# Two pairs' last score chunks on four 64x64 tiles, and the seventh group's q squared before its k

## The chip, the cores and the metric

One core of one Trainium2 chip. The metric is device microseconds of one execution of the whole kernel; times are medians over several executions, with the lowest and highest behind them. The profile shows one of these executions from inside; its span is 1.8 us shorter than that execution's time. TensorE's granted clock is reported for each execution: 1.00 is full speed, and one stretch of about 3.4 us at half speed lowers the mean of a 587 us span by about 0.003. A "hole" is a stretch in which TensorE starts nothing; the profile's own count of it (idle time, in square brackets) is 0.1 to 0.2 us shorter than the distance from start to start less the usual distance, and the text says which one it means where that matters.

## The reference

Cosine attention of 8 batches x 12 heads x 448 positions x 64, then a low-rank token mixer with a channel mixer of two matmuls.

```python
q_n = q / (norm(q) + 1e-6);  k_n = k / (norm(k) + 1e-6)
attn = softmax(q_n @ k_n.T / tau)
x = heads_side_by_side(attn @ v)              # 8 x 448 x 768
u = x + ((x.T @ U) @ V).T                     # U 448x32, V 32x448
return u + relu(u @ w_ch1) @ w_ch2            # 768 -> 3072 -> 768
```

## The kernel before

Heads go through in 48 pairs, 0 to 47, two heads of 64 side by side in 128 partitions. Pairs 0 to 5 are the first batch. q, k and v are loaded in groups of one or two pairs; the seventh group holds pairs 10 and 11, the eighth pairs 12 and 13, the ninth 14 and 15, the tenth 16 and 17. A group is squared on GpSimd, reduced and inverted on VectorE, and scaled to bf16; from pair 12 on the scaled q and k are transposed by DMA instead of by TensorE. After the start nearly all loads, stores and transposes go out from one queue, SyncE's; the mixer's weights (w1 and w2, of `w_ch1` and `w_ch2`) are issued by GpSimd. The code is shortened: arguments shown as `...` and the calls that only keep count of time (`est`) are left out.

```python
def step_T(b, p):
    if not by_dma(b * NP + p):                # by_dma: pair >= 12
        pe_T(b, p); evict_T(b, p); return
    gi, j = group_of[(b, p)]
    nc.sync.dma_start_transpose(out=new_qkT(b, p)..., in_=norm[gi][0][:, j, ...]...)

def pe_S(b, p, c):                            # scores, chunk c of the keys
    sc = psum.tile([128, 2, 512], FP, name="sc", tag="ps_sc", bufs=2)
    if c == 3:                                # last: 64 keys of each head, one wide matmul
        nc.tensor.matmul(out=sc[:, 0, 0:S], lhsT=t[:, 1, 384:512], rhs=t[:, 0, 0:S], ...)
        return
    for h in range(2):                        # two row tiles side by side
        r = slice(64 * h, 64 * h + 64)
        nc.tensor.matmul(out=sc[:, h, 0:S], lhsT=t[r, 1, c * 128:(c + 1) * 128], rhs=t[r, 0, 0:S], ...)
# (cut)
for gi in range(5, len(groups)):
    # at: the places (pair, step) of square q, square k, cast v, reduce q, reduce k, root
    # when: of the inversion and the four scalings
    elif m == NP + 4:                         # the seventh group
        at = [(NP + 2, 0), (NP + 2, 0), (NP + 2, 6), (NP + 2, 3), (NP + 2, 4), (NP + 2, 5)]
        when = [(NP + 2, 6), (NP + 2, 6), (NP + 3, 0), (NP + 3, 2)]
    # (cut)
    put(*at[1], lambda g=g: g.square(1))      # k
    put(*at[0], lambda g=g: g.square(0))      # q; same place: stays behind k
    # (cut)
    put(m - 6, 4, lambda gi=gi: load(gi, "q", nc.sync))
    put(m - 5, 5, lambda gi=gi: load(gi, "k", nc.sync))
    put(m - 4, 3, lambda gi=gi: load(gi, "v", nc.sync))
    if by_dma(m):
        put(m - 1, -1 if m > 2 * NP else 2, lambda m=m: T(m))
        put(m - 1, 0 if m > 2 * NP else 4, lambda m=m: T(m + 1))
```

## Time and profile before

| | before |
|---|---|
| time, median of 3 (range) | 590.51 us (589.85 to 591.66) |
| span of the profiled execution | 587.6 us |
| TensorE busy | 574.8 us, 98% |
| longest hole of TensorE | 2.65 us from start to start (2.49 idle), at 69.2 to 71.9 us, then 3.4 us at half clock |
| wide last-chunk matmuls | 48, each 0.19 us from start to start |

TensorE is the bound, so time is read as a sequence of TensorE starts: work removed shortens it, and so does a hole removed, as long as nothing further on stops TensorE at a fixed moment.

### The profile page before, as it was taken

What the parts mean: (1) busy time and instruction counts of PE and PEld (TensorE: products, weight loads), DVE (VectorE), ACT (ScalarE), POOL (GpSimd) and SP (SyncE); (2) the same over time, 40 slices, a digit from 0 to 9 for tenths busy, and PEclk for the clock granted to TensorE, in tenths of its full rate; (3) what the DMA queues carried; (4) which work ended last, traced back from release to release, by engine and by line L of the source; (5) the groups of instructions that cost most, each with busy time, mean ns of one, the idle gap of its engine ahead of it and who ended that gap; (6) DMA issues with size and microseconds to landing.
All of it is one profiled execution on the core that took longest, in us unless ns stands there. A gap on an engine that the chain in (4) does not pass through costs nothing.

```text
span 587.6 us, 11561 instructions
## 1 busy us (share of the span) xinstructions
PE 574.8 (98%) x4729; PEld 328.9 (56%) x4729; DVE 254.3 (43%) x500; ACT 263.6 (45%) x452; POOL 187.8 (32%) x160
## 2 busy tenths in 40 slices
PE   7999899999999999999999999999999999999997
PEld 6665456655555555554555555655555545555564
DVE  7875644534444437425344255633355242220011
ACT  5966455356324555346433465345442465214300
POOL 9674456504135045224053153252251410000000
PEclk9999999999999999999999999999999999999999
DMA  6999999456275464574565763773545631222022
GB/s 165 204 227 233 240 236 227 119 117 135 73 162 139 107 145 113 132 162 108 94 151 121 157 132 86 147 162 85 135 108 133 131 65 26 56 61 46 7 48 55
DMA packets 138581, 74.20 MB, mean 126 GB/s; under 512 B 85568, under 2 KB 138352, under 8 KB 138528
## 3 DMA queue, kind: packets, MB, share of 16 engines
q1 hardware_dynamic: 128256, 62.77, 47.3%
q0 software_dynamic: 9728, 10.18, 10.2%
q8 instruction: 37, 0.61, 0.4%
q10 hardware_dynamic: 544, 0.51, 0.3%
q14 instruction: 16, 0.13, 0.1%
HBM read 52.19 MB, written 11.01 MB: 108 GB/s over the span
## 4 chain that ended last, share of the span: by engine, by line
PE 89%; DMA 6%; DVE 1%; SPq 1%; ACT 1%; issue 0%; DVEq 0%; ACTq 0%; POOLq 0%
PE mp L512 38%; PE mp L485 34%; PE sc L318 5%; PE av L356 3%; DMA qst<-in_q_dram 3%; PE up L356 2%; DMA kst<-in_k_dram 2%; PE sc L312 1%; DMA vst<-in_v_dram 1%; PE av L349 1%; PE up L349 1%; PE up L442 1%; PE av L455 1%; PE tp L288 1%; ACT E L329 0%
## 5 line engine op out<-in xcount | busy, mean ns | idle before, releaser
L512 PE MATMUL mp<-w_sb,relu 128*128 128x384 bf16 x1344 | 236.1, 326 | 0.0
L512 PEld LDWEIGHTS <-relu 128*128 128x128 bf16 x1344 | 125.4, 98 | 91.3 <-issue 14.3
L485 PEld LDWEIGHTS <-w_sb 128*128 128x128 bf16 x1152 | 107.6, 98 | 101.5 <-issue 10.5
L329 ACT ACTIVATE E<-sc 128x896 bf16<-128x896 f32 x144 | 124.6, 916 | 65.4 <-PE sc L318 64.8
L489 ACT ACTIVATE relu<-mp 128x448 bf16<-128x448 f32 x167 | 90.9, 544 | 136.6 <-PE mp L485 136.6
L259 POOL TENSOR_TENSOR qk<-kst,inv 128x512 bf16<-128x512 f32 x41 | 49.6, 1226 | 259.5 <-DVE inv L253 259.5
L485 PE MATMUL mp<-uE,w_sb 128*128 128x448 bf16 x576 | 119.8, 354 | 0.0
L485 PE MATMUL mp<-uO,w_sb 128*128 128x448 bf16 x576 | 115.6, 353 | 0.0
L530 DVE TENSOR_TENSOR o_sb<-mp,ut 128x384 f32<-128x384 f32 x50 | 27.8, 556 | 122.6 <-PE mp L512 122.6
L239 DVE TENSOR_REDUCE ss<-sq 128x16 f32<-128x1024 f32 (+1 forms) x50 | 56.8, 1165 | 3.5 <-POOL sq L234 2.8
L367 DVE RECIPROCAL rd<-av 128x4 f32<-128x4 f32 x54 | 9.7, 181 | 90.9 <-PE av L356 90.9
L234 POOL TENSOR_TENSOR sq<-kst 128x1024 f32<-128x1024 f32 (+1 forms) x23 | 43.9, 1912 | 13.3 <-DMA kst<-in_k_dram 6.8
L259 DVE TENSOR_TENSOR qk<-qst,inv 128x512 bf16<-128x512 f32 x42 | 45.7, 1094 | 0.5
L356 PEld LDWEIGHTS <-E 128*128 128x128 bf16 x1152 | 45.0, 97 | 0.0
L234 POOL TENSOR_TENSOR sq<-qst 128x1024 f32<-128x1024 f32 x21 | 42.8, 2040 | 5.0 <-DMA qst<-in_q_dram 5.0
L318 PE MATMUL sc<-qkT 64*128 64x448 bf16 x288 | 41.7, 358 | 1.2 <-ACT E L326 0.6
L326 ACT ACTIVATE E<-sc 128x448 bf16<-128x448 f32 x48 | 26.0, 541 | 28.7 <-PE sc L312 28.7
L267 POOL CAST v<-vst 128x1024 bf16<-128x1024 f32 (+1 forms) x25 | 28.5, 1142 | 13.1 <-DMA vst<-in_v_dram 7.6
L491 DVE TENSOR_SCALAR relu<-mp 128x448 bf16<-128x448 f32 x25 | 15.6, 623 | 33.8 <-PE mp L485 33.5
L356 PE MATMUL av<-v,E 128*128 128x65 bf16 x648 | 29.1, 193 | 0.0
L349 PEld LDWEIGHTS <-E 128*128 128x128 bf16 x192 | 17.9, 98 | 15.3 <-DVE uO L460 0.8
L367 DVE RECIPROCAL rd<-up 128x4 f32<-128x4 f32 x36 | 6.5, 182 | 44.9 <-PE up L356 44.9
(93 smaller groups left out, 328.3 us busy)
## 6 DMA issues: line engine op xcount, KB each, us to landing
out_dram<-o_sb SPq DMA_DIRECT2D x109, 96.0 KB, 2.2
w_sb<-in_moe_w_ch_dram POOLq DMA_DIRECT2D x8, 1152.0 KB, 26.2
qst<-in_q_dram SPq DMA_DIRECT2D x23, 256.0 KB, 4.0
vst<-in_v_dram SPq DMA_DIRECT2D x46, 128.0 KB, 2.7
kst<-in_k_dram SPq DMA_DIRECT2D x44, 128.0 KB, 2.7
qst<-in_q_dram SPq DMA_DIRECT2D x23, 192.0 KB, 4.0
vst<-in_v_dram SPq DMA_DIRECT2D x46, 96.0 KB, 2.6
kst<-in_k_dram SPq DMA_DIRECT2D x44, 96.0 KB, 2.7
```

Of the source, the lines that this page charges most:

```text
L234: nc.gpsimd.tensor_mul(sq[:, 0:self.nh * 4, :], self.flat(t), self.flat(t))
L239: nc.vector.reduce_sum(self.ss[:, j, 0:self.nh * 4], self.sq[j][:, 0:self.nh * 4, :], axis=AX.X)
L259: eng.tensor_mul(qks[self.gi % 2][:, j, i, :, :, :], t[:, 2 * j:2 * j + 2, :, :].rearrange("p h c d -> p c h d"), iv.unsqueeze(3).to_broad ...
L267: nc.gpsimd.tensor_copy(out=self.flat(v65[self.s])[:, :, 0:D], in_=self.flat(vst[self.s]))
L318: nc.tensor.matmul(out=sc[:, h, 0:S], lhsT=t[r, 1, c * 128:(c + 1) * 128], rhs=t[r, 0, 0:S], start=True, stop=True)
L329: nc.scalar.activation(out=e[:, 2 * c:2 * c + 2, 0:S], in_=sc[:, :, 0:S], func=AF.Exp)
L349: nc.tensor.matmul(out=av[:, i, :, :], lhsT=e[:, 6, ic * 128:(ic + 1) * 128], rhs=vv[:, 2 * j:2 * j + 2, 3, :], start=(i == 0), stop=False ...
L356: nc.tensor.matmul(out=av[:, i, h, :], lhsT=e[:, 2 * c + h, ic * 128:(ic + 1) * 128], rhs=vv[:, 2 * j + h, c, :], start=False, stop=(i == ...
L485: nc.tensor.matmul(out=mp, lhsT=w1_sb[:, cc, f * 128:(f + 1) * 128], rhs=u[:, cc, 0:S], start=(cc == 0), stop=(cc == CC - 1))
L489: nc.scalar.activation(out=relu[:, f, o:o + S], in_=mp, func=AF.Relu)
L512: nc.tensor.matmul(out=mp, lhsT=relu[:, f, r0:r0 + 128], rhs=w2_sb[:, f, half * HC:(half + 1) * HC], start=(f == 0), stop=(b > 0 and f == ...
L530: nc.vector.tensor_add(o.rearrange("p (k d) -> p k d", d=128), mp.rearrange("p (k d) -> p k d", d=128), ut_of[(b, half)][:, :, c, :])
```

## The change

Three things. From pair 14 on, the last score chunks of two pairs are computed together by four 64x64 matmuls on the four quarters of the array, in two banks (separate pieces) of PSUM, the memory that TensorE writes to, instead of one wide matmul for each pair. So that each head's last keys lie on the right partitions, k and v of the middle two heads of a group are loaded mirrored. And the seventh group's q is squared first, its k second.

```diff
+    def step_S3(b, p):
+        for i, (nm, tag) in enumerate((("av", "ps_av"), ("up", "ps_x"))):
+            t = qkT[(b, p + i)]
+            bank = psum.tile([128, 512], FP, name=nm, tag=tag, bufs=1)
+            sc_of[(b, p + i, 3)] = bank.unsqueeze(1)
+            for h in range(2):
+                r, o = slice(64 * h, 64 * h + 64), 64 * (h ^ i)
+                nc.tensor.matmul(out=bank[o:o + 64, 0:S], lhsT=t[r, 1, 384 + o:448 + o],
+                                 rhs=t[r, 0, 0:S], start=True, stop=True)
+        # (cut)
+        for i in range(2):
+            exp_S(b, p + i, 3)
# (cut: order of an even pair's steps)
             order = [
+                (2, now and (lambda: (step_S3(*pairs[n]), Sc(n, 0, 1)))),
                 (2, lambda: V(n - 1, 0)),
-                (2, now and (lambda: Sc(n, 0, 1))),
                 (2, lambda: (V(n - 1, 1), X2(n - 1))),
-                (2, now and (lambda: Sc(n, 3))),
# (cut: the seventh group)
-            at = [(NP + 2, 0), (NP + 2, 0), (NP + 2, 6), (NP + 2, 3), (NP + 2, 4), (NP + 2, 5)]
-            when = [(NP + 2, 6), (NP + 2, 6), (NP + 3, 0), (NP + 3, 2)]
+            at = [(NP + 2, 0), (NP + 2, 1), (NP + 2, 6), (NP + 2, 3), (NP + 2, 5), (NP + 2, 6)]
+            when = [(NP + 3, 0), (NP + 3, 0), (NP + 3, 1), (NP + 3, 3)]
# (cut: a buffer E3 for the exponentials of the last chunks, with its own fills of ones on
#  GpSimd; mirrored loads; V_raw under another tag; two reciprocal buffers instead of four)
```

More of the change, by code (lines that the diff above doesn't have):

```diff
@@ L98 @@
         for lst in (kst, vst):
-            nc.vector.memset(lst[i][64:128, 0:NG:2, 3, :], 0.0)
-            nc.vector.memset(lst[i][0:64, 1:NG:2, 3, :], 0.0)
+            nc.vector.memset(lst[i][64:128, 0:NG:3, 3, :], 0.0)
+            nc.vector.memset(lst[i][0:64, 1:3, 3, :], 0.0)
     ident = const.tile([128, 128], BF, name="ident")
@@ L104, with last_of @@
         nc.gpsimd.memset(t[:, :, :, D:D + 1], 1.0)
-        nc.gpsimd.memset(t[64:128, 0:NG:2, 3, D:D + 1], 0.0)
-        nc.gpsimd.memset(t[0:64, 1:NG:2, 3, D:D + 1], 0.0)
-    E = []
+        nc.gpsimd.memset(t[64:128, 0:NG:3, 3, D:D + 1], 0.0)
+        nc.gpsimd.memset(t[0:64, 1:3, 3, D:D + 1], 0.0)
+    E, E3 = [], []
     for i in range(2):
-        t = const.tile([128, 7, 512], BF, name=f"E{i}")
+        t = const.tile([128, 6, 512], BF, name=f"E{i}")
         nc.gpsimd.memset(t[:, :, S:512], 1.0)
         E.append(t)
+        t = const.tile([128, 2, 512], BF, name=f"E3{i}")
+        nc.gpsimd.memset(t[:, :, S:512], 1.0)
+        E3.append(t)
+    def last_of(b, p):
+        n = b * NP + p
+        return E3[n // 2 % 2][:, n % 2, :]
     U_raw = const.tile([128, 4, R], FP, name="U_raw")
     U_sb = const.tile([128, 4, 128], BF, name="U_sb")
-    V_raw = work.tile([128, S], FP, name="V_raw", tag="XT", bufs=2)
+    V_raw = work.tile([128, S], FP, name="V_raw", tag="ut", bufs=2)
     A_sb = [const.tile([128, 128], BF, name=f"A_sb{i}") for i in range(2)]
@@ L200, in load @@
         x, t = (k, kst[s]) if what == "k" else (v, vst[s])
-        ev, od = slice(h0, h0 + nh, 2), slice(h0 + 1, h0 + nh, 2)
-        engs[0].dma_start(out=dst(t, L, slice(0, nh, 2), 4), in_=src(x, ev, 0, 256, 4))
-        engs[1].dma_start(out=dst(t, U2, slice(0, nh, 2), 3), in_=src(x, ev, 256, 448, 3))
-        engs[2].dma_start(out=dst(t, L, slice(1, nh, 2), 3), in_=src(x, od, 0, 192, 3))
-        engs[3].dma_start(out=dst(t, U2, slice(1, nh, 2), 4), in_=src(x, od, 192, 448, 4))
+        m = min(3, nh)
+        ou, mi = slice(h0, h0 + nh, 3), slice(h0 + 1, h0 + m)
+        engs[0].dma_start(out=dst(t, L, slice(0, nh, 3), 4), in_=src(x, ou, 0, 256, 4))
+        engs[1].dma_start(out=dst(t, U2, slice(0, nh, 3), 3), in_=src(x, ou, 256, 448, 3))
+        engs[2].dma_start(out=dst(t, L, slice(1, m), 3), in_=src(x, mi, 0, 192, 3))
+        engs[3].dma_start(out=dst(t, U2, slice(1, m), 4), in_=src(x, mi, 192, 448, 4))
     norm = {}
@@ L320, in pe_S @@
         est.pe(0.25)
+    def step_S3(b, p):
[7 more added lines that the diff above has]
+                                 rhs=t[r, 0, 0:S], start=True, stop=True)
+        est.pe(0.19)
+        for i in range(2):
+            exp_S(b, p + i, 3)
     def exp_S(b, p, c):
@@ L325, in exp_S @@
         if c == 3:
-            nc.scalar.activation(out=e[:, 6, 0:S], in_=sc[:, 0, 0:S], func=AF.Exp)
+            nc.scalar.activation(out=last_of(b, p)[:, 0:S], in_=sc[:, 0, 0:S], func=AF.Exp)
             est.act(0.56)
@@ L348, in pe_V @@
             ic = 2 * half + i
-            nc.tensor.matmul(out=av[:, i, :, :], lhsT=e[:, 6, ic * 128:(ic + 1) * 128],
+            nc.tensor.matmul(out=av[:, i, :, :], lhsT=last_of(b, p)[:, ic * 128:(ic + 1) * 128],
                              rhs=vv[:, 2 * j:2 * j + 2, 3, :],
@@ L365, in divide_V @@
         av = av_of[(b, p, half)][:, 0:4 * (D + 1)].rearrange("p (i h d) -> p i h d", i=2, h=2)
-        rd = work.tile([128, 4, 1], FP, name="rd", tag="rd", bufs=4)
+        rd = work.tile([128, 4, 1], FP, name="rd", tag="rd", bufs=2)
         nc.vector.reciprocal(out=rd, in_=av.rearrange("p i h d -> p (i h) d")[:, :, D:D + 1])
@@ L793 @@
             order = [
+                (2, now and (lambda: (step_S3(*pairs[n]), Sc(n, 0, 1)))),
                 (2, lambda: V(n - 1, 0)),
-                (2, now and (lambda: Sc(n, 0, 1))),
                 (2, lambda: (V(n - 1, 1), X2(n - 1))),
-                (2, now and (lambda: Sc(n, 3))),
+                (2, None),
                 (3, lambda: (A2(n - 2), now and (Sc(n, 2), Sc(n + 1, 0)))),
@@ L816 @@
             (2, lambda: V(n - 1, 0)),
-            (2, lambda: Sc(n, 3)),
+            (2, None if n > FIRST2 + 1 else (lambda: Sc(n, 3))),
             (2, lambda: (V(n - 1, 1), X2(n - 1))),
```

## The prediction

> **What bounds the kernel now.** I read the first part of the page (busy shares), then the costliest groups, then the TensorE timeline of one late pair of heads, then the waits, then the stretches with their clock. The page's first part, and two of its groups:
>
> ```profile
> span 587.6 us, 11561 instructions
> PE 574.8 (98%) x4729; PEld 328.9 (56%) x4729; DVE 254.3 (43%) x500; ACT 263.6 (45%) x452; POOL 187.8 (32%) x160
> ...
> L318 PE MATMUL sc<-qkT 64*128 64x448 bf16 x288 | 41.7, 358 | 1.2 <-ACT E L326 0.6
> ...
> L312 PE MATMUL sc<-qkT 128*128 128x448 bf16 x48 | 16.9, 353 | 0.6 <-ACT E L329 0.6
> ```
>
> TensorE is busy 98% of the span, every other engine under half. So only two things can move the end: TensorE work taken out, and the 12.8 us (587.6 - 574.8) in which it waits. The mean of 353 ns for L312 is the latency of one matmul, not its price: matmuls are pipelined, so the price is the distance from one start to the next. The TensorE timeline of a late even pair shows it (start, length, count):
>
> ```profile
> 380.84 0.81 PE L512 MATMUL mp<-w_sb,relu 128*128 128x384 bf16 x4
> 381.49 0.35 PE L312 MATMUL sc<-qkT 128*128 128x448 bf16 x1
> 381.68 2.11 PE L512 MATMUL mp<-w_sb,relu 128*128 128x384 bf16 x12
> ...
> 386.49 0.55 PE L318 MATMUL sc<-qkT 64*128 64x448 bf16 x4
> 386.88 0.35 PE L455 MATMUL av<-V_sb,A_sb 64*128 64x448 bf16 x1
> 386.88 0.35 PE L455 MATMUL up<-V_sb,A_sb 64*128 64x448 bf16 x1
> 387.16 1.15 PE L512 MATMUL mp<-w_sb,relu 128*128 128x384 bf16 x6
> ```
>
> The wide last-chunk matmul takes 0.19 us (381.49 to 381.68). Two row-tiled ones at L455 start together and the next wide one follows after 0.28 us. Over all such places in the trace, medians of start to start: wide to wide 162 ns at 384 columns and 189 ns at 448; wide to a 64-row form 259 and 285 ns, so 96 ns more; 64-row to wide 282 ns, about 95 more than the 186 ns from one 64-row pair to the next (L318 to L455); from the 128x32 form (L442) to the 64-row form 152 ns, again 96 more than its 56. Every change of tile form costs 96 ns, staying in one costs nothing.
>
> The waits and the DVE, GpSimd and TensorE timelines around the one long hole give the second point:
>
> ```profile
> PE av L389 <- DVE X L368: 2.5, 1, 2.5
> ...
> 70.05 1.22 DVE L239 TENSOR_REDUCE ss<-sq 128x16 f32<-128x1024 f32 x1 [2.76 <-POOL sq L234]
> 71.19 0.17 DVE L367 RECIPROCAL rd<-av 128x4 f32<-128x4 f32 x1
> 71.39 0.42 DVE L368 TENSOR_TENSOR X<-av,rd 128x256 bf16<-128x256 f32 x1
> ...
> 66.28 1.89 POOL L234 TENSOR_TENSOR sq<-kst 128x1024 f32<-128x1024 f32 x1 [6.40 <-DVE rd L367]
> 68.13 1.88 POOL L234 TENSOR_TENSOR sq<-qst 128x1024 f32<-128x1024 f32 x1
> ...
> 68.08 1.30 PE L485 MATMUL mp<-uE,w_sb 128*128 128x448 bf16 x6
> 71.87 0.58 PE L389 MATMUL av<-X,U_sb 128*128 128x128 bf16 x4 [2.49 <-DVE X L368]
> ```
>
> ```profile
> 69.20:71.90 2.70, 0.21 (x2) 0.03 (x1) 1.81 (x4) 0.55 (x1) 1.85 (x2) 1.00 1.22 239
> 71.90:75.30 3.40, 3.40 (x17) 1.57 (x17) 1.58 (x3) 2.42 (x5) 0.99 (x1) 0.50 1.22 242
> ```
>
> Backward: the matmul at 71.87 waits for X, X stands in VectorE's queue behind the reduction of squared q, that waits for GpSimd's square of q, which comes second, after the square of k. The second fence (stretch, length, busy times, granted clock, DMA) shows what follows: the 2.7 us hole, then 3.4 us at clock 0.50. The "DVE rd" named before the square of k at 66.28 I do not believe: the transfers of k were issued at 51.3 to 55.5 and took 10.6 us or more to land, so the last lands at 66.1; the second q transfer, issued at 49.80, took 12.6 and was there at 62.4. The square waited for k while q lay ready. Excess of start to start over the normal distance, summed from 71.87 to 75.4: 2.65 us hole plus 1.4 us of half clock, 4.05 us. It is the eighth pair's stretch, and the squares are the seventh group's. Besides the start (first 41 us) there are no other holes over 0.6 us.
>
> **What the skill says.** "TensorEngine Tiling (Array Packing)", Key Properties: changing the tiling mode drains TensorE, changing the tile does not; the trace agrees, 96 ns against none. "TensorE: Matmul & The Clock Gate", Part 3 (The mechanism): tiles run concurrently, starts about 4 ns apart; here L318's two tiles start 4 ns apart (median). The same page, Part 1 (What's actually happening): after an idle window of about 3.4 us the clock halves; here 2.65 us of waiting were followed by 3.4 us at 0.50. "PSUM — Partial Sum Buffer", PSUM bank collisions: column tiles may write one bank at once, row tiles may not, measured there per bank and 32-partition quadrant. No run so far shows two row tiles in one bank on different partitions, which is what the change does.
>
> **The change part by part.**
> 1. Last chunks. Pairs 14 to 47, 34 of 48, lose their wide matmul: 34 x 189 ns = 6.43 us less. Instead 17 times four 64x64 matmuls for two pairs, each on its own tile. If they stream together as L318's pairs do, 186 ns + 3 x 4 = about 0.20 us: 17 x 0.20 = 3.4 us more. They stand directly before the first two chunks of scores (64x128), so the visit wide to 64-row to wide becomes wide to 64x64 to 64x128 to wide: one form change more, 17 x 96 ns = 1.6 us. Sum: -6.4 + 3.4 + 1.6 = -1.4 us. All of it is on TensorE, thus on the path.
> 2. The exponentials of these chunks stay 34 of 541 ns on ScalarE (45% busy), but two now come together ahead of two of 917 ns, about 3.0 us in a row. The first attention-times-values product now needs the bank that the first of them reads: it comes after about 0.5 us of scores and one mixer step of 1.0 to 1.1 us, 1.8 us after the new matmuls; the exponential is over at about 0.35 + 0.54 = 0.9 us, or 1.4 with a 0.54 us relu ahead. Nothing added.
> 3. The transposed q and k of the second pair are needed one pair earlier. The transposes are issued 5.7 us or more ahead of an even pair's start and take 3.1 to 5.5 us to land: just enough.
> 4. Mirrored middle heads: the same transfers with other head steps; nothing. V_raw in another buffer, two reciprocal buffers instead of four: nothing. The ones columns take four GpSimd fills instead of two: from fills of 448, 384 and 128 elements (468, 444, 205 ns) 0.36 us more at GpSimd's start, where it works without a gap until 14 us; I take 0.2 us for the span.
> 5. Seventh group, q first: q's square can run 62.4 to 64.3, before VectorE is at its reduction (free at 67.3). Reduction to 68.5, then the division, 0.6 us: X at 69.1, and TensorE comes to it at 69.2. The hole goes and with it the half clock: -4.05 us. k's square stays at about 66.2 to 68.1, its reduction is moved later by one place. What follows comes 4 us earlier into a time of loaded DMA (to about 97 us): w2's pieces landed 78.8, 88.7 and 95.2 us against first uses, shifted, of about 82, 98 and 100, enough; but pair 12's transpose was just in time before (issued 97.3, used at 101.3 with a small wait) and would now be issued near 93 among other transfers. I take +0.5 us.
>
> Sum: -1.4 + 0.2 - 4.05 + 0.5 = -4.75 us, from 590.5 to 585.8. So the larger part should come from the smallest edit, the order of two squares.
>
> **The rivals.**
> A. Tiles in one bank serialise. Then a visit is two passes of 0.19 us: 17 x 0.19 = 3.2 us more, the first part turns from -1.4 to +1.8, the time is 589. For it: the skill's sentence on row tiles and banks. Against it: the partitions differ, and each half of a bank gets one tile at a time. 10%.
> B. The step from 64x64 to 64x128 costs nothing, since the rows stay 64: another -1.6 us, 584.2. The trace shows only that 128x32 to 64x128 costs 96 ns, where both dimensions change. 20%.
> C. New waits: the values product waits for the exponential, or the mixer's banks for relus behind 3 us of exponentials. For it: two more buffers tied to ScalarE; against: the estimates in 2, and that VectorE can take relus. 0.2 us at 17 places would be 3.4 us, time 589. 10%.
> D. The hole stays, since the wait was for VectorE as the profile names it, or the transfers land later: 590. 10%.
>
> **Range and chances.** 2% is 11.8 us, more than twice what all parts give together, and no rival loses that much. Both gains full with B and no late transpose: 583.7; one of A, C or D: 588 to 590. Prediction 585.8, range 583.4 to 588.4. Faster by over 2%: 1%; within 2%: 98%; slower: 1%.
>
> **What would show it.** In the new trace: the four 64x64 starts within about 12 ns, the next 64x128 start some 290 ns after them (190 if B, near 480 if A); 14 L312-like matmuls left; TensorE busy less by some 3 us (1.4 from the tiles, 1.4 from the clock); no stretch at clock 0.50 near 72 us; the square of q starting near 62.4 and no wait of the X product over 0.3 us. I am wrong if the hole is still there, if it moves to pair 12's transpose or to 97 us with over 1 us, or if waits of TensorE for exponentials sum to over 1 us.

## The result, and the profile after

| | before | after |
|---|---|---|
| time beside each other, median of 4 (range) | 590.18 us (589.67 to 591.66) | 589.29 us (588.49 to 589.51) |
| span of the profiled execution | 587.6 | 586.7 |
| TensorE busy | 574.8 | 571.8 |

The ratio is 0.9978 (95%: 0.9957 to 0.9999). A ratio is the mean time of one kernel's fast runs over that of the other's in the same rounds, so not quite the ratio of the medians. The interval only just leaves out 1. The change gains 0.9 us where 4.75 were predicted, and 589.29 lies outside the range of 583.4 to 588.4.

The head of the page after. TensorE is busy 3.0 us less, and yet the span is only 0.9 us shorter, so it waits more than before (14.9 us instead of 12.8):

```profile
span 586.7 us, 11660 instructions
PE 571.8 (97%) x4763; PEld 327.2 (56%) x4763; DVE 259.4 (44%) x503; ACT 260.9 (44%) x449; POOL 187.7 (32%) x162
```

The tiles in the TensorE timeline after (start, length, engine, line, operation, count). The four 64x64 matmuls of L340 stream together, two banks 10 ns apart in these rounded starts, and the 64x128 scores of L328 follow 0.31 us later:

```profile
400.95 0.38 PE L340 MATMUL av<-qkT 64*64 64x448 bf16 x2
400.96 0.38 PE L340 MATMUL up<-qkT 64*64 64x448 bf16 x2
401.27 0.55 PE L328 MATMUL sc<-qkT 64*128 64x448 bf16 x4
```

The place of the old hole: the X product (L413) now starts at 71.64 directly behind the mixer step, without a wait. GpSimd squares q at 62.73, and k when it has landed, at 66.96. The stretch that held the hole (length, busy times of TensorE, weight loads, VectorE, ScalarE and GpSimd, granted clock, DMA share, GB/s) is full:

```profile
70.51 1.30 PE L509 MATMUL mp<-uE,w_sb 128*128 128x448 bf16 x6
71.64 0.39 PE L413 MATMUL av<-X,U_sb 128*128 128x128 bf16 x4
```

```profile
62.73 1.89 POOL L244 TENSOR_TENSOR sq<-qst 128x1024 f32<-128x1024 f32 x1 [3.00 <-DVE rd L391]
66.96 1.89 POOL L244 TENSOR_TENSOR sq<-kst 128x1024 f32<-128x1024 f32 x1 [2.34 <-DVE uO L443]
```

```profile
69.20:71.90 2.70, 2.70 (x31) 1.73 (x29) 2.67 (x5) 1.04 (x3) 1.04 (x1) 1.00 1.24 237
28.70:32.10 3.40, 3.40 (x32) 2.47 (x31) 1.41 (x4) 1.86 (x4) 1.95 (x2) 0.52 1.12 258
```

The second of these stretches shows that the half clock is not gone: it now lies at 28.7 to 32.1. It follows a hole at the start, where the first product of attention and values of pair 2 waits for the cast of v (TensorE, then GpSimd, before):

```profile
25.41 0.29 PE L349 MATMUL av<-v,E 128*128 128x130 bf16 x2
```

```profile
23.48 1.03 POOL L267 CAST v<-vst 128x1024 bf16<-128x1024 f32 x1 [3.17 <-DMA vst<-in_v_dram]
```

and after, where the same v landed at 26.0 instead of 23.3 us:

```profile
27.21 0.28 PE L373 MATMUL av<-v,E 128*128 128x130 bf16 x2 [1.65 <-POOL v L277]
```

```profile
26.13 1.03 POOL L277 CAST v<-vst 128x1024 bf16<-128x1024 f32 x1 [5.61 <-DMA vst<-in_v_dram]
```

And at pair 12. Before, its first scores (L318) follow the matmul ahead of them without a stop. The transposes that they need were issued at 97.33 (the queue of SyncE), and the view of their line gives the time from issue to landing:

```profile
100.95 0.35 PE L414 MATMUL up<-V_sb,A_sb 128*128 128x448 bf16 x1
101.28 0.55 PE L318 MATMUL sc<-qkT 64*128 64x448 bf16 x4
```

```profile
97.33 2.75 SPq L303 DMA_TRANSPOSE qkT<-qk  x2
```

```profile
DMA to landing us min/median/max: 3.3/3.6/3.9
```

After, TensorE is there at 99.5, 1.8 us earlier, and stands still until 101.61. The transposes were issued 1.8 us earlier too, at 95.53, behind loads of v and q, and took 2.1 us longer to land (the same three views):

```profile
99.15 0.35 PE L438 MATMUL up<-V_sb,A_sb 128*128 128x448 bf16 x1
101.61 0.55 PE L328 MATMUL sc<-qkT 64*128 64x448 bf16 x4 [2.11 <-DMA qkT<-qk]
```

```profile
88.92 0.65 SPq L212 DMA_DIRECT2D vst<-in_v_dram  x1
...
92.63 0.59 SPq L206 DMA_DIRECT2D qst<-in_q_dram  x1
...
95.53 4.90 SPq L313 DMA_TRANSPOSE qkT<-qk  x2
```

```profile
DMA to landing us min/median/max: 5.4/5.7/6.0
```

**Where the time went.** I compared the start of the first values product of every pair in the two traces (after less before; the starts of pair 2 are the two lines above, those of pair 47 are 513.34 and 512.38):

| from | to | change of the lag, us | what lies there |
|---|---|---|---|
| start | pair 3 | +3.00 | the hole at 25 to 27 us and the half clock behind it; 0.57 of it is won back by pair 7 |
| pair 7 | pair 8 | -4.22 | the hole near 72 us and its half clock are gone |
| pair 8 | pair 10 | 0.00 | |
| pair 10 | pair 11 | +2.13 | the wait for pair 12's transposes |
| pair 12 | pair 47 | -1.30 | the tiles |
| | sum | -0.96 | with the 0.57 |

The seventh group gave what was predicted (-4.05) and a little more, the tiles nearly what was predicted (-1.4). What was not predicted is a loss of 2.4 us (3.00 - 0.57) at the start and one of 2.1 us at pair 12.

**Theories.** W: the transposes of pair 12 land at about 101 us whenever TensorE arrives, because the queue ahead of them is full until then; pair 12 is a wall, and everything won ahead of it is lost there. F (rival): the two added fills on GpSimd (four instead of two) delay the start and cause its hole. R (rival): the start hole is chance, a race of v's transfer with another. H (rival to W): it isn't the transposes, but the clock, which halves somewhere in any case. W and either F or R can both hold, since they speak of different places.

### The profile page after: what moved, and what is told of

The parts are those of the page before. It is cut to its first block, busy times and chain, and to the rows that moved or that the text cites. A ratio compares the mean times of both kernels' runs of the same rounds, so it can differ in the third digit from the quotient of the medians.

```text
span 586.7 us, 11660 instructions
## 1 busy us (share of the span) xinstructions
PE 571.8 (97%) x4763; PEld 327.2 (56%) x4763; DVE 259.4 (44%) x503; ACT 260.9 (44%) x449; POOL 187.7 (32%) x162
## 4 chain that ended last, share of the span: by engine, by line
PE 88%; DMA 6%; issue 1%; DVE 1%; SPq 1%; ACT 1%; POOL 1%; ACTq 0%; POOLq 0%; DVEq 0%
PE mp L536 36%; PE mp L509 36%; PE sc L328 5%; PE av L380 3%; DMA vst<-in_v_dram 2%; PE up L380 2%; DMA qst<-in_q_dram 2%; DMA qkT<-qk 1%; PE av L373 1%; PE av L340 1%; PE up L373 1%; PE up L466 1%; PE av L479 1%; PE tp L298 1%; DVE qk L269 0%
## 5 line engine op out<-in xcount | busy, mean ns | idle before, releaser
L536 PE MATMUL mp<-w_sb,relu 128*128 128x384 bf16 x1344 | 233.3, 326 | 0.0
L513 ACT ACTIVATE relu<-mp 128x448 bf16<-128x448 f32 x164 | 89.1, 543 | 130.7 <-PE mp L509 130.7
L509 PE MATMUL mp<-uE,w_sb 128*128 128x448 bf16 x576 | 117.5, 353 | 0.0
L509 PE MATMUL mp<-uO,w_sb 128*128 128x448 bf16 x576 | 114.2, 353 | 0.0
L515 DVE TENSOR_SCALAR relu<-mp 128x448 bf16<-128x448 f32 x28 | 17.5, 623 | 79.8 <-PE mp L509 79.4
L269 DVE TENSOR_TENSOR qk<-qst,inv 128x512 bf16<-128x512 f32 x42 | 46.9, 1122 | 0.6
L328 PE MATMUL sc<-qkT 64*128 64x448 bf16 x288 | 41.6, 357 | 3.3 <-DMA qkT<-qk 2.1
L350 ACT ACTIVATE E<-av 128x448 bf16<-128x448 f32 x17 | 9.2, 541 | 47.4 <-PE up L340 47.4
L470 ACT CAST A_sb<-up 128x128 bf16<-128x128 f32 x18 | 4.7, 263 | 46.0 <-PE up L466 46.0
```

The costliest lines, as they stand in the source:

```text
L269: eng.tensor_mul(qks[self.gi % 2][:, j, i, :, :, :], t[:, 2 * j:2 * j + 2, :, :].rearrange("p h c d -> p c h d"), iv.unsqueeze(3).to_broad ...
L509: nc.tensor.matmul(out=mp, lhsT=w1_sb[:, cc, f * 128:(f + 1) * 128], rhs=u[:, cc, 0:S], start=(cc == 0), stop=(cc == CC - 1))
L513: nc.scalar.activation(out=relu[:, f, o:o + S], in_=mp, func=AF.Relu)
L536: nc.tensor.matmul(out=mp, lhsT=relu[:, f, r0:r0 + 128], rhs=w2_sb[:, f, half * HC:(half + 1) * HC], start=(f == 0), stop=(b > 0 and f == ...
```

## The experiments

Each was run beside the kernel before on the same chip; all gave correct results. Four groups, each group on one chip: the first four kernels, then e7 to e10, e11 to e13, and e14 to e16.

| run | kernel | median us (range) | ratio to before [95%] | pair 12's first scores | last pair's first values | between |
|---|---|---|---|---|---|---|
| before | (its profile, from the start) | 590.51 (589.85 to 591.66) | | 101.28 | 513.34 | 412.06 |
| after | the change | 589.29 (588.49 to 589.51) | 0.9978 [0.9957, 0.9999] | 101.61 | 512.38 | 410.77 |
| e1 | before + order | 590.70 (589.16 to 591.68) | 1.0010 [0.9991, 1.0028] | 101.00 | 513.05 | 412.05 |
| e2 | after - order | 587.64 (586.90 to 588.42) | 0.9959 [0.9942, 0.9975] | 100.83 | 511.58 | 410.75 |
| e3 | after, fills on VectorE | 590.67 (587.67 to 591.01) | 1.0003 [0.9980, 1.0026] | 100.68 | 512.82 | 412.14 |
| e4 | after, pairs 12, 13 turned on TensorE | 585.85 (585.42 to 586.79) | 0.9931 [0.9915, 0.9947] | 97.99 | 509.21 | 411.22 |
| e7 | e4 - order | 588.32 (586.92 to 589.26) | 0.9968 [0.9953, 0.9982] | 101.83 | 513.05 | 411.22 |
| e8 | before + turned on TensorE | 589.11 (588.28 to 590.99) | 0.9990 [0.9973, 1.0007] | 100.47 | 512.98 | 412.51 |
| e9 | e8 + order | 587.33 (585.97 to 592.80) | 0.9965 [0.9935, 0.9995] | 97.58 | 510.09 | 412.51 |
| e10 | e4, tiles twice | 589.36 (588.52 to 592.52) | 0.9996 [0.9976, 1.0015] | 98.08 | 512.50 | 414.42 |
| e11 | after, two loads later | 584.88 (583.80 to 585.39) | 0.9904 [0.9886, 0.9921] | 98.39 | 509.15 | 410.76 |
| e12 | e4, v ahead of weights | 588.31 (584.87 to 590.08) | 0.9972 [0.9954, 0.9989] | 97.46 | 508.67 | 411.21 |
| e13 | e11, v ahead of weights | 585.07 (584.33 to 588.18) | 0.9917 [0.9896, 0.9938] | 98.47 | 509.24 | 410.77 |
| e14 | after, again | 588.71 (587.22 to 589.37) | 0.9973 [0.9957, 0.9989] | 100.65 | 511.42 | 410.77 |
| e15 | e11 - order | 586.54 (585.98 to 588.08) | 0.9941 [0.9926, 0.9956] | 99.48 | 510.25 | 410.77 |
| e16 | after - order (e2's text) | 587.79 (587.48 to 588.30) | 0.9961 [0.9948, 0.9974] | 100.73 | 511.50 | 410.77 |

The last three columns are starts in us in the profiled execution and their difference. They are the strongest reading: from pair 12 on, a kernel takes 412.05 or 412.06 us without the tiles and 410.75 to 410.77 with them, in whichever run (0.45 more where pair 12's and 13's transposes are work of TensorE, and 1.4 more in e3, which has a half clock there). So the tiles are worth 1.29 us, and everything else that differs between two runs has happened before pair 12's first scores.

### e1 and e2: each part of the change alone

```diff
 # e1: before, with only this
-            at = [(NP + 2, 0), (NP + 2, 0), ... (NP + 2, 4), (NP + 2, 5)]
+            at = [(NP + 2, 0), (NP + 2, 1), ... (NP + 2, 5), (NP + 2, 6)]
 # (and the line of when); e2: the change with these two lines as before
```

> The kernel before with nothing but the seventh group's new order. Theory (a wall): the 2.65 us hole near 72 us and its half clock go, but pair 12's transposes land at about 101 us whatever comes before them, so the first scores of pair 12 start at 101 to 102 us after a wait of 3 to 4 us, and the time is that of the kernel before within 0.6 us (589.6 to 590.8). Rival (the start ate the gain): without the late start of the changed kernel the gain of 4 us stays, about 586.5, and pair 12 waits under 1 us.

> The changed kernel with the seventh group's order put back. Theory: the hole near 72 us is back (some 2.5 us or less, since it is set by transfers and the start's delay hides in it), pair 12 waits under 0.5 us, and what is left is the tiles' gain of 1.1 to 1.4 us: 588.8 to 589.3, so the same as the whole change. Rival: the order is worth its own 2 us or more, and this is at 590 or slower.

The order alone gives nothing (590.70 against 589.84 of before on that chip), though the larger predicted gain lies in it. That is the time that the wall foretold, but e1's trace doesn't show the wall: pair 12 waits 0.4 us, not the expected 3 to 4, because a start hole (1.51 us before the values product at 26.88, with the fills as in before), the half clock behind it and a wait of 1.25 us at 64.0 us for a scaled q or k had already made TensorE late. What e1 does give is the first sign against F, since it has none of the added fills. The tiles with the old order give 2.2 us, more than was expected of them and more than with the new order: in e2's trace X waits 1.24 us near 72 us and pair 12 1.34 us (under 0.5 was expected), no half clock follows either, and pair 12 starts 0.45 us earlier than in before, which adds to the tiles' 1.3. The part that was worth 4.05 us on paper makes the change no faster.

### e3: the added fills on another engine

```diff
         t = const.tile([128, 2, 512], BF, name=f"E3{i}")
-        nc.gpsimd.memset(t[:, :, S:512], 1.0)
+        nc.vector.memset(t[:, :, S:512], 1.0)
```

> The changed kernel with the two fills of the new tiles on VectorE instead of GpSimd, so that GpSimd's start is as before. Theory (fills shift the loads into the weights' transfer): the hole of 1.7 us at 25 to 27 us goes, the first 60 us are as in the kernel before within 0.5 us, but pair 12 then waits 4 to 5 us and the time stays at 588.8 to 589.6. Rival 1: the start's hole is chance and is still there. Rival 2: no wall, and the time falls by 2 to 3 us to about 586.5.

The start hole is gone from its profile, so TensorE reaches pair 12 earlier than in the change, and waits longer there; this wait is followed by a half clock (TensorE timeline, then the stretch):

```profile
100.68 0.93 PE L328 MATMUL sc<-qkT 64*128 64x448 bf16 x4 [3.02 <-DMA qkT<-qk]
```

```profile
100.60:103.80 3.20, 3.12 (x12) 1.27 (x13) 0.00 (x0) 1.73 (x2) 0.00 (x0) 0.53 0.65 178
```

TensorE came to pair 12 1.8 us earlier than in after; 0.9 of that became wait (3.02 against 2.11, where 4 to 5 was expected) and the half clock took another 1.4: a hole taken away ahead of the wall came back at it, which speaks for W. The runs sort by their clock, 587.67 at 0.999, 588.91 at 0.997 and 590.45 to 591.01 at 0.994 or 0.995; a stretch at half clock costs 1.2 to 1.5 us in these traces (1.20 behind pair 2 in after, 1.37 in e3, 1.54 in before against e8). Its median, 590.67, is above the 588.8 to 589.6 expected. On F alone the run would have gained what the start lost, and it didn't. That the hole went could still be the fills or chance; e14 returns to it.

### e4: the wall taken away by TensorE

```diff
+    def turned_by_dma(n):
+        return n >= 2 * NP + 2
     def step_T(b, p):
-        if not by_dma(b * NP + p):
+        if not turned_by_dma(b * NP + p):     # and so at the three places that order T
```

> The changed kernel with pairs 12 and 13 transposed on TensorE instead of by DMA. It costs TensorE 2 x 0.46 us and takes the wait of 2.1 us at 101 us away: 1.2 us faster than the changed kernel, about 588.1. If instead something else sets pair 12 (its scales, the banks), the time is 0.9 us longer, about 590.2.

Pairs 12 and 13 are now transposed by TensorE, 16 more matmuls. The scores of pair 12 start 2.7 us earlier than in e3 on the same chip, with no wait:

```profile
97.99 0.55 PE L332 MATMUL sc<-qkT 64*128 64x448 bf16 x4
```

The time is 585.85, what was predicted for the change itself (585.8), and the six runs lie within 1.4 us of each other, with clocks of 0.998 and above, so none with a whole stretch at half clock. It came out better than expected because the start hole, which I had counted in, is absent from its profile.

### e7, e8 and e9: does the order pay once the wall is gone?

e7 is e4 with the seventh group's old order, e8 is before with the two pairs' transposes on TensorE, e9 is e8 with the new order.

> The tiles, pairs 12 and 13 transposed on TensorE, the seventh group in its old order. Theory (the order's gain was real and only hidden by the wall): the hole near 72 us is back and nothing at 101 us hides it, so it is 1.5 to 4 us slower than e4_turn_on_pe, 587.4 to 589.9. Rival (the order is worth nothing in itself): within 0.5 us of e4, about 586.

> The kernel before with nothing but pairs 12 and 13 transposed on TensorE. Before had no wait to speak of at pair 12, so this takes nothing away and adds 2 x 0.46 us of TensorE work: 590.3 to 591.0, 0 to 1 us slower than before. If it is faster than before by over 1 us, the wall cost the kernel before too.

> The kernel before with the seventh group's new order and pairs 12 and 13 on TensorE, no tiles. Theory: order and wall only pay together: -4.05 + 0.9 from the kernel before, 586.5 to 587.5, while e1_order_only alone gave 0 and e8_turn_only alone gives 0 or less. The difference to e4_turn_on_pe, 1.0 to 1.4 us, is what the tiles are worth. Rival: the hole near 72 us only moves to another place and the time stays above 589.

The order is worth 2.2 us with the tiles (ratio 0.9931 against 0.9968, e4 against e7, on two chips; e7's profiled execution had a start hole and 6.8 us at half clock, so that its X product doesn't wait at all, two more had clocks of 0.994 and 0.997, and its three runs at a clock of 0.999 or 1.0 are 1.1 to 2.0 us above e4's median) and 1.5 to 1.8 us without (e9 against e8, same chip, intervals that overlap; one of e9's six runs took 592.80, and why is not known). The move of the transposes alone gains next to nothing (e8), since the hole at 72 us remains ahead of it. So neither the order alone (e1) nor the turn alone (e8) gives anything that can be told from zero, and the two together give 2.1 us by the ratio, 2.6 by the medians: two holes in a row, of which the second takes what the first gives back. e8's X product waited 2.52 us and was not followed by a half clock, unlike before's of 2.49; so the predicted 4.05 us was the case with half clock, and 2.65 the case without.

### e10: what four tiles cost

```diff
-        for i, (nm, tag) in enumerate(...):   # two banks, each its two matmuls
+        for i in (0, 1, 0, 1):                # e4, every set of four matmuls run twice
```

> As e4_turn_on_pe, with each set of four 64x64 matmuls done twice over the same result. If the four stream together the second set starts about 190 to 200 ns after the first one's start, and the time rises by 17 x 0.2 = 3.3 us to about 589.1. If two row tiles in one bank are served in turn, it starts 380 ns after, and the time rises by 6.4 us. The 306 ns from the last of the four to the next 64x128 start should stay: what it has over 190 is the form change.

e10 lies 3.5 us above e4 in time, and 3.2 us (414.42 - 411.22) in its trace, 0.188 us for each of the 17 additional sets: one pass in a row, for four tiles at once. The TensorE timeline:

```profile
400.12 0.38 PE L347 MATMUL av<-qkT 64*64 64x448 bf16 x2
400.13 0.38 PE L347 MATMUL up<-qkT 64*64 64x448 bf16 x2
400.34 0.35 PE L347 MATMUL av<-qkT 64*64 64x448 bf16 x2
400.35 0.35 PE L347 MATMUL up<-qkT 64*64 64x448 bf16 x2
400.63 0.55 PE L332 MATMUL sc<-qkT 64*128 64x448 bf16 x4
```

The second set starts 203 ns (median) after the first set's last, and the 64x128 matmul 282 ns after the second set's last. A first pass after a change of form is thus about 20 ns longer than the 186 ns of one in a row, and then the change to 64x128 costs 96 ns more. In the change, with one set, it is 9 ns for the four starts (3 ns apart) and 306 ns to the next form: 315 against 2 x 189 = 378, so 63 ns a visit instead of the predicted 84, x17 = 1.07 us. Most of the rest of the measured 1.29: two waits of 0.2 us of the values product (233.4 and 369.9 us in before) are gone, and two of 0.115 us (213.8 and 349.8 us, of the mixer) are new.

### e11: the wall taken away by the queue

```diff
-        put(*at[2], lambda g=g: g.values())
+        put(*((12, 3) if gi == 8 else at[2]), lambda g=g: g.values())
-            put(m - 6, 4, lambda gi=gi: load(gi, "q", nc.sync))
+            put(*((11, 5) if gi == 9 else (m - 6, 4)), lambda gi=gi: load(gi, "q", nc.sync))
-            put(m - 4, 3, lambda gi=gi: load(gi, "v", nc.sync))
+            put(*((11, 5) if gi == 8 else (m - 4, 3)), lambda gi=gi: load(gi, "v", nc.sync))
```

> The changed kernel, with v of the ninth group and q of the tenth (0.9 MB that nobody needs before 105 us) loaded after pair 12's and 13's transposes instead of ahead of them. Theory (the transposes of pair 12 stand behind loads and weights, and that is the wall): the transposes land 2 to 3.5 us earlier, near 98 to 99 us, pair 12 waits under 1 us, no half clock there, and the time falls by 1.5 to 3 us to 586.5 to 587.8. Rival (the weights in the other queue alone set it, or the transposes' own length): landing stays at 100.7 to 101.6 and the time at 589 to 590.7.

In the change, the v of the ninth group and the q of the tenth are issued from 88.9 to 93.9 us, just ahead of the transposes, and neither reaches TensorE before pair 14's values products at 144.7 us. Here they go out behind the transposes, which remain transfers (TensorE, SyncE's queue, and the time to landing):

```profile
98.39 0.55 PE L328 MATMUL sc<-qkT 64*128 64x448 bf16 x4
```

```profile
94.44 2.81 SPq L313 DMA_TRANSPOSE qkT<-qk  x2
```

```profile
DMA to landing us min/median/max: 3.2/3.3/3.4
```

Issued at 94.44, the transposes land in 3.3 us, and the scores start at 98.39 without a wait, although this execution had a start hole (0.91 us idle). 584.88 us, 4.9 below before: the best of all kernels here, with four runs. e15, below, has the same queue, and its transposes took 3.1 to 3.3 us. That settles what the wall is made of: not the transposes as such, but the transfers in front of them. It isn't gone, though, but lies earlier: in e13, which has this queue too and issued them at 93.8, they took 4.1 to 4.7 us and pair 12 waited 0.7. No run takes the weights away from there, so their part in it isn't known. The Trainium skill, "DMA: Bandwidth & Descriptors", section "Issuing engines are not separate DMA queues", says that DMAs of all issuing engines run on the same 16 DMA engines and interleave; the trace agrees, for with SyncE's two loads out of the way the last piece of w2, which GpSimd issued at 55.2, landed at 95.4 us here, and at 98.2 in the change (issued at 55.8).

### e14, e16 and e15: the change again, and the order once more

e14 is the change word for word, e16 is e2 word for word, e15 is e11 with the old order.

> The changed kernel itself, on the same chip as the two that follow. If the new order costs more than it brings while pair 12 waits for its transposes, this is 1 to 3 us slower than e16_change_old_order: 588.5 to 591, with a mean clock of 0.994 to 0.997 in its slower runs (one or two windows at half clock).

> The same text as e2_tiles_only, beside the changed kernel this time. Theory: the two holes, near 72 and near 101 us, are each too short to halve the clock, so it lies at 587 to 588.5 and below the changed kernel by 1 us or more. Rival: what e2 showed was the chip or chance, and the two kernels agree within 0.6 us.

> e11_light_queue with the old order. With no wall at pair 12 the order should be worth what the hole near 72 us takes: 1.4 to 4 us slower than e11_light_queue, 586.3 to 588.9. If it is within 0.5 us of e11, the light queue alone made the gain and the order none.

e14's profile, the same kernel text as after, has no start hole. v landed in time; the fills are the same. So R and not F alone: the start hole is a race that v's last transfer (issued by SyncE at 19.5 to 20.0 us) loses in some executions against the first slice of weights (issued by GpSimd at 19.4 to 20.0), and it also occurs with before's start (e1). The traces sort by the head start of the weights. In the five with a start hole (after, e1, e7, e11, e16) the weights were issued 0.13 to 0.24 us ahead of v's last transfer, which then took 5.5 to 6.5 us to land; in the nine others with this order the head start was at most 0.11 us or the weights came later, and v took 2.9 to 4.4 us. That the fills make the longer head start more likely isn't ruled out by so few traces. In e14 TensorE therefore comes to pair 12 earlier still, and gives all of it back:

```profile
100.65 0.55 PE L328 MATMUL sc<-qkT 64*128 64x448 bf16 x4 [2.83 <-DMA qkT<-qk]
```

Its median is 588.71 (how many of its six runs had a start hole isn't known), just outside the predicted range, and its two runs at a clock of 0.998 and 0.999 (587.22, 587.51) are inside. The profiled one had no half clock to speak of and still waited 2.8 us at pair 12, so H falls: the clock comes on top of the wall and isn't the wall.

Beside it, the change with the old order is not slower but, if anything, faster by 0.9 us (587.79; the intervals overlap). Its X product waits at 72 us for only 1.04 us:

```profile
71.17 0.38 PE L413 MATMUL av<-X,U_sb 128*128 128x128 bf16 x4 [1.04 <-DVE X L392]
```

That hole is another wall of the same kind, set by the landing of k: TensorE came there later than in before, and k had landed earlier (its square starts at 65.58 instead of 66.28). So the hole that I priced at 4.05 us is not a fixed sum either; it is the distance between TensorE's arrival and a transfer's. With the light queue the order pays again: 0.9904 (e11) against 0.9941 (e15), 2.2 us, with intervals that don't touch, on two chips.

### e12 and e13: v ahead of the first weights

```diff
-  ... ex20 S21 V10 ex21 w1_0 V11 X10 S22 Te3 root3 val2
+  ... ex20 S21 V10 ex21 V11 X10 S22 Te3 root3 val2 w1_0      # order of the start, w1_0: weights
```

> As e4_turn_on_pe, with the first slice of the mixer's weights asked for after the cast of the third group's v instead of before it. Theory (the start's hole at 25 to 27 us is a race of v's last transfer against that slice, won or lost by chance): v lands by 22 us, the hole can't occur, and all runs lie close together at a clock of 0.998 or more: 585.4 to 586.4, e4's times without its spread. If the later weights make another hole, it is 1 us or more slower than e4.

> The changed kernel with both: v before the weights' first slice, and the light queue at pair 12, transposes still by DMA. If both causes are as thought, no hole over 1 us is left at 25, 72 or 101 us and TensorE is spared e4's 0.9 us of transposes: 584.9 to 586. If the weights come later and the wall with them, 586.5 to 588.

A miss. e12's profiled execution has no start hole (v landed at about 22.7 us) and is its fastest, 584.87, but the other five lie between 587.74 and 590.08, and e4, without the edit, is steadier and 2.5 us faster (on another chip). Putting v first moves all weights later, and something else may then wait in most executions; the profile caught the one in which nothing did, so where the others lose their time stays open. Put on e11, the edit changes the median by 0.2 us, which is nothing; its profile shows a new wait of 1.1 us (start to start) at 42.5 us and 0.7 at pair 12.

## Why the prediction was wrong

- **What bounds the kernel:** right. TensorE's starts set the end. Its busy time fell by 3.0 us, as foretold (some 3), but since the half clock only moved from 72 to 29 us, this figure doesn't confirm the two terms of 1.4 behind it.
- **Part 1, the last chunks, -1.4:** right in mechanism, measured -1.29. The four tiles start 3 ns apart, 306 ns to the next form where 290 was foretold. The visit saves 63 ns, not 84; the first pass after a change of form is longer by some 20 ns.
- **Rivals A and B:** both fell. Two row tiles in one bank do not serialise (that would have been near 480 ns), and the step from 64x64 to 64x128 isn't free (that would have been 190).
- **Part 2 and rival C, waits for exponentials:** right, next to nothing added. The score matmuls wait for exponentials 1.3 us in total after (0.9 at L328, 0.4 at L322); that is over the 1 us that I had set as a sign of error, but before had 1.5 by the same count (0.9 at L318, 0.6 at L312).
- **Part 5, the seventh group, -4.05:** right where it lies: -4.22 between pairs 7 and 8 (2.65 of hole and 1.57 of half clock, where 1.4 was taken), q's square at 62.7 against a predicted 62.4, no wait of the X product. But it was no gain of the kernel. The landing times of w2 in this part (78.8, 88.7 and 95.2 us) were misread: before's trace has 80.1, 89.3 and 96.8. Nothing hung on it, as no matmul with w2 waits in after.
- **Part 4, fills, +0.2:** not to be seen. The pairs before the hole lag 0.2 to 0.3 us in after and e14, but as much in e8 and e9, which have no added fills. The 2.4 us that after lost at the start are a race that I had not seen, because the one profile of before had won it (with a head start of 0.06 us for the weights).
- **The step that failed: "pair 12's transpose was just in time before (issued 97.3, used at 101.3 with a small wait) and would now be issued near 93 among other transfers. I take +0.5 us."** It was issued at 95.5 and took 5.4 to 6.0 us where before's took 3.3 to 3.9; the wait was 2.1 us in after, 2.8 in e14 and 3.0 in e3, with a half clock on top in e3. The sentence has the reason in it and not its size: I moved the issue forward and left the landing time nearly as it was. But "just in time" means that two chains ended together, TensorE's and the transfers', and of the second only its tail moves with TensorE. The transfers in front (v of the ninth, q of the tenth group, the second half of w2, whose last piece landed at 96.8 to 98.4 us) did not drain sooner because TensorE was ahead. In the seven traces with the full queue (before, after, e1, e2, e3, e14, e16) the first of the two transposes was issued anywhere from 93.7 to 97.3 us and landed from 100.6 to 101.6.
- **Does that explain the miss?** In numbers: with +2.9 for +0.5 (e14, no start hole) and -1.3 for -1.4 the sum becomes 585.8 + 2.4 + 0.1 = 588.3, against 588.71 measured. The other 0.4, and the 0.6 up to the first result of 589.29, are of the size of the two chance events, the start hole and a half clock. And without the wall the same kernel takes 585.85 (e4) or 584.88 (e11).
- **The list of what would show me wrong** named it: "if it moves to pair 12's transpose ... with over 1 us". The range did not: its upper end, 588.4, had one of the rivals in it, and none of the rivals was the full return of the gain at the next place where a transfer was just in time.

What stays open: what shifts the two issues of the start by a tenth of a microsecond, so that v loses its race in five of the fourteen profiles that have it; what decides whether a hole of 1.5 to 3 us brings a half clock; how much of the wall is w2's; and where e12's slower runs lose their time.

## What to carry to other kernels

A wait of zero at a transfer is not slack: before counting a gain on the bound engine, walk forward to every later place where it meets a transfer, and ask when that transfer would land if the engine were early; all that is won ahead of the latest such landing is lost there, and sometimes a half clock with it. Where a transfer is just in time, look at what stands ahead of it in its queue and is needed later: putting two loads behind two transposes was worth more here (3.8 to 4.4 us, e11 against e14 and after) than the whole change. And one profile shows one throw: a start that raced well in the only profile of before cost 2.4 us in the first profile of after, with no cause in the change that could be shown.

## What the Trainium skill lacked or had wrong

- "TensorEngine Tiling (Array Packing)", Key Properties, says that a change of tiling mode drains TensorE and gives no price. Here it is 94 to 97 ns a change at 384 and 448 columns, whether one dimension of the tile changes or both, and the first pass in the new form takes 203 ns (64x64) or 196 (64x128) instead of 186.
- "PSUM — Partial Sum Buffer", PSUM bank collisions, quotes that different row tiles can't access one bank at the same time, while what it measured itself, an error, was for two row tiles in one bank and the same 32 partitions. Here two tiles that differ in rows and in columns wrote the two partition halves of one bank, starts 3 ns apart, 34 banks an execution, with correct results in every run: on disjoint partitions the quoted sentence is too wide.
- "TensorE: Matmul & The Clock Gate", Part 1, gives an idle window of about 3.4 us for the half clock. Here holes of 1.51 us (e1), 1.65 (after), 2.49 (before) and 3.02 (e3) came with 3.4 us at 0.5, which began in the hole or at most 1.4 us behind it, and holes of 1.69 us (e16), 2.52 (e8) and 2.83 (e14) did not: shorter idle times can be enough, and what decides it no run here shows.
- "DMA: Bandwidth & Descriptors" gives a bandwidth for DMA transposes, but no landing time for one issued behind other transfers. Here the same transpose took 3.2 to 3.4 us behind a light queue (e11) and up to 6.7 us behind a full one (e14).
